# A gated-GELU feed-forward on one core: a 4-byte tile moves into the padding of the identity's tile, so that the SBUF pools start at multiples of 512 bytes

## The chip, the core and the metric

The kernel runs on one core of a Trainium2 chip. The metric is the device time of one execution in microseconds. Five engines work side by side and wait for each other through semaphores: PE (TensorE, matrix products), DVE (VectorE), ACT (ScalarE), POOL (GpSimd) and SP (SyncE, which here issues nearly all DMA transfers). PE appears twice in the profile: PE is the matrix product, PEld is the loading of the stationary operand ("the weights") that comes before each product. A product streams the other operand ("the moving operand") past those weights.

## The reference

```
B, S, Dm, Df = 1, 2048, 1024, 3584          # all inputs bfloat16
g = jnp.einsum("bsd,df->bsf", x, w_gate)
u = jnp.einsum("bsd,df->bsf", x, w_up)
h = _gelu(g) * u                            # tanh form of GELU
return jnp.einsum("bsf,fd->bsd", h, w_down)
```

## The kernel before, in words

The 2048 rows of x are taken in two passes (L1140) of two blocks of 512 rows each. For the first two products the 3584 hidden columns are cut into 14 units of 256 columns (`w_gate` and `w_up` are loaded by `load_w`, L151). The kernel does not multiply block by block in the plain way: it cuts rows, columns and the contraction in two and uses a scheme with seven products in place of eight. The scheme needs sums and differences of blocks: of x (t1 to t4, made by DVE, `sums_t`, L168), of the weights (s1 to s4, made mostly by POOL, `sums_s`, L183), and copies in 32 bits (tb, sa, made by ACT). They are kept in 32 bits (`f32r` in the code; the profile writes f32 or fp32r). So PE has two kinds of products of 128x512: bf16 with bf16, and f32 with f32. `matmul` (L144) issues every one of them, so all carry line L145. Units 4 to 13 go a level deeper (`pair0` L375, `pair1` L519). Then `down` (L898) multiplies the hidden values by `w_down` with the same scheme; in the last pass it calls `apart` (L866), whose products have five blocks K1, K3, K4, K22, K2 as weights (`load_ti`, L772). K1 and K2 are put into the two tiles `xT0` and `xT1`, which x no longer needs; K22, K3 and K4 go into tiles of the pool "w". Later in the same pass `make73` (L666) puts the first eight of fourteen moving blocks `tb` into `xT1` and `xT0` again (L675), and the other six into slots of the pool "k" (L679).

The order on PE, DVE, POOL, SP and ACT is that of the program text (L82 and the blocks under it); an agenda written by hand (L804 to L838) gives the step at which each load and each sum of `down` is made. Data passes from engine to engine by semaphore waits that the language derives from the tiles.

The pools of SBUF are opened in a fixed order (L83 to L89): x, m, h, w, k, s. Each takes the bytes behind the one before it, in every partition, rounded up to 32 bytes. Constants and a reserved part take the first 16,512 bytes. The pool x holds `hx` (1024 bytes, L294), `ident` (256 bytes, L996), `xT0` and `xT1` (8192 bytes each, L93) and `seen` (4 bytes, L1085). `ident` is the identity with which the first four row blocks of x are transposed (L1011). `seen` is written by POOL alone (`pool_behind`, L198) and read by nobody: the copy of one value makes POOL wait until DVE has made a tile, twice in the whole program (L1213).

From the sizes follow the places in the built program, in bytes of a partition (in brackets the rest after division by 512):

| tile or pool | before | after |
|---|---|---|
| hx | 16512 (128) | 16512 (128) |
| ident, or small | 17536 (128) | 17536 (128) |
| xT0, xT1 | 17792, 25984 (384) | 17920, 26112 (0) |
| seen | 34176 (384) | in small |
| m, two tiles of 6144 | 34208 (416) | 34304 (0) |
| hT | 46496 (416) | 46592 (0) |
| forms, hL | 83360 (416) | 83456 (0) |
| w, three tiles of 8192 | 103840 (416) | 103936 (0) |
| k, 36 slots of 2048 | 128416 (416) | 128512 (0) |
| s, 13 slots of 2048 | 202144 (416) | 202240 (0) |

Within a pool every tile is a multiple of 512 bytes long, and every operand of PE that is cut out of an f32 tile starts a multiple of 512 bytes behind the tile's start (128 columns of 4 bytes). So one rest holds for all f32 operands of a pool.

Of the kernel before, what the change touches and what calls it, by code (L numbers as in the profile page):

```python
# [10 lines left out]
def kernel(  # L11
# [26 lines left out]
    P = nc.NUM_PARTITIONS  # L38
    bf16 = mybir.dt.bfloat16
    f32 = mybir.dt.float32  # L40
# [42 lines left out]
    xpool = ctx.enter_context(tc.tile_pool(name="x", bufs=1))  # L83
# [909 lines left out]


    warm = nc.const_aps.tensor(1.0, [P, N], bf16)
    ident = xpool.tile([P, P], bf16, name="ident")  # L996
    make_identity(nc, ident)

    def load_x(c):
# [82 lines left out]
        s.make("sa", "s2", "s4")  # L1082
        t.make("t1")

    seen = xpool.tile([P, 1], f32, name="seen")  # L1085

    def rest_of_0(part):
        if part == 0:
# [244 lines left out]
```

## Time and profile before

| what | value |
|---|---|
| time, median of 3 runs | 535.11 us (534.42 to 536.17) |
| time of the profiled execution | 534.34 us |
| its span, from the first to the last instruction | 532.5 us |
| granted TensorE clock | 1.00 |
| PE busy | 527.3 us, 99% of the span, 2375 products |
| DVE, ACT, POOL busy | 404.6, 302.2, 268.2 us |
| DMA moved | 126.09 MB, mean 237 GB/s |

The profiled execution took 1.84 us more than its span (534.34 less 532.5): that is what lies ahead of the first and behind the last profiled instruction. The profile says how long each engine was busy, which chain of work ended last, and what ended each wait. Busy PE does not tell how densely the products follow each other, since they overlap; for that one takes the starts of products that follow each other.

### The profile page before, as it was taken

What the parts mean: (1) busy time and instruction counts of PE and PEld (TensorE: products, weight loads), DVE (VectorE), ACT (ScalarE), POOL (GpSimd) and SP (SyncE); (2) the same over time, 40 slices, a digit from 0 to 9 for tenths busy, and PEclk for the clock granted to TensorE, in tenths of its full rate; (3) what the DMA queues carried; (4) which work ended last, traced back from release to release, by engine and by line L of the source; (5) the groups of instructions that cost most, each with busy time, mean ns of one, the idle gap of its engine ahead of it and who ended that gap; (6) DMA issues with size and microseconds to landing.
All of it is one profiled execution on the core that took longest, in us unless ns stands there. A gap on an engine that the chain in (4) does not pass through costs nothing.

```text
span 532.5 us, 7751 instructions
## 1 busy us (share of the span) xinstructions
PE 527.3 (99%) x2375; PEld 373.7 (70%) x2375; DVE 404.6 (76%) x646; ACT 302.2 (57%) x545; POOL 268.2 (50%) x259
## 2 busy tenths in 40 slices
PE   8999999999999999999999999999999999999997
PEld 4568686867677774588886676767668674587885
DVE  2998768787777786938799877576576679789895
ACT  2557686868586851015556866566656651074580
POOL 1169976979797970000002989695978900000000
PEclk9999999999999999999999999999999999999999
DMA  9695318686777599999999799954383399499983
GB/s 246 153 254 170 87 60 295 199 296 199 236 226 257 186 361 369 387 293 267 225 276 295 246 281 350 324 153 140 99 225 97 118 370 353 159 342 337 217 191 131
DMA packets 140729, 126.09 MB, mean 237 GB/s; under 512 B 31632, under 2 KB 119184, under 8 KB 140560
## 3 DMA queue, kind: packets, MB, share of 16 engines
q1 hardware_dynamic: 136336, 124.55, 76.9%
q10 hardware_dynamic: 4352, 1.05, 1.5%
q8 instruction: 19, 0.31, 0.3%
q14 instruction: 22, 0.18, 0.1%
HBM read 86.38 MB, written 31.06 MB: 221 GB/s over the span
## 4 chain that ended last, share of the span: by engine, by line
PE 97%; DVE 2%; DMA 1%; SPq 0%; issue 0%; ACT 0%
PE bank L145 96%; DVE q L121 1%; DMA xn<-in_x_dram 1%; DVE xT L121 1%; SPq L1004 0%; PE bank L1011 0%; DVE st L854 0%; ACT st L853 0%
## 5 line engine op out<-in xcount | busy, mean ns | idle before, releaser
L124 POOL TENSOR_TENSOR s<-w 128x512 fp32r<-128x512 bf16 x102 | 117.4, 1169 | 47.5 <-DMA w<-in_w_gate_dram 37.0
L145 PE MATMUL bank<-t,s 128*128 128x512 f32 x528 | 126.3, 392 | 0.0
L145 PEld LDWEIGHTS bank<-t,s 128*128 128x128 f32 x528 | 99.0, 188 | 21.6 <-POOL s L124 0.3
L145 PE MATMUL bank<-xT,w 128*128 128x512 bf16 (+1 forms) x504 | 110.4, 376 | 0.0
L145 PEld LDWEIGHTS <-w 128*128 128x128 bf16 x504 | 47.8, 98 | 58.2 <-issue 4.2
L213 ACT ACTIVATE g<-sum 128x512 f32<-128x512 f32 x81 | 51.5, 636 | 60.1 <-DVE sum L121 59.3
L138 ACT COPY p<-bank 128x512 f32<-128x512 f32 x98 | 55.0, 589 | 46.6 <-PE bank L145 46.5
L121 DVE TENSOR_TENSOR hT<-g,bank 128x512 bf16<-128x512 f32 x72 | 49.0, 687 | 17.8 <-ACT g L213 12.2
L124 POOL TENSOR_TENSOR s<-w,s 128x512 fp32r<-128x512 bf16 x50 | 57.8, 1173 | 0.4
L124 POOL TENSOR_TENSOR s<-s,w 128x512 fp32r<-128x512 f32 x50 | 57.3, 1165 | 0.2
L145 PE MATMUL bank<-q 128*128 128x512 f32 x224 | 56.3, 391 | 0.1
L121 DVE TENSOR_TENSOR bank<-bank,p 128x512 f32<-128x512 f32 x74 | 51.3, 695 | 5.7 <-PE bank L145 5.1
L145 PE MATMUL bank<-t,sa 128*128 128x512 f32 x216 | 54.9, 397 | 0.0
L199 POOL COPY seen<-t 128x1 f32<-128x1 f32 x2 | 0.4, 183 | 107.8 <-DMA ti<-td 91.7
L145 PE MATMUL bank<-tb,s 128*128 128x512 f32 x216 | 54.3, 393 | 0.0
L145 PEld LDWEIGHTS bank<-q 128*128 128x128 f32 x224 | 42.1, 188 | 9.6 <-DVE xT L121 0.6
L145 PEld LDWEIGHTS bank<-t,sa 128*128 128x128 f32 x216 | 40.6, 188 | 9.1
L145 PEld LDWEIGHTS bank<-tb,s 128*128 128x128 f32 x216 | 40.5, 188 | 9.0 <-POOL s L124 0.3
L121 DVE TENSOR_TENSOR sum<-bank,p 128x512 f32<-128x512 f32 x54 | 37.0, 685 | 12.2 <-PE bank L145 11.1
L138 ACT COPY u<-bank 128x512 f32<-128x512 f32 x62 | 35.4, 595 | 17.5 <-PE bank L145 14.1
L133 ACT CAST tb<-raw 128x512 fp32r<-128x512 bf16 x20 | 12.0, 628 | 38.0 <-DMA raw<-in_w_down_dram 31.1
L133 ACT CAST sa<-w 128x512 fp32r<-128x512 bf16 x54 | 30.7, 617 | 3.4 <-DMA out_dram<-st 3.4
(123 smaller groups left out, 732.5 us busy)
## 6 DMA issues: line engine op xcount, KB each, us to landing
raw<-in_w_down_dram SPq DMA_DIRECT2D x72, 256.0 KB, 5.8
w<-in_w_gate_dram SPq DMA_DIRECT2D x27, 512.0 KB, 4.6
w<-in_w_up_dram SPq DMA_DIRECT2D x27, 512.0 KB, 6.1
td<-m SPq DMA_DIRECT2D x11, 768.0 KB, 5.3
q<-td SPq DMA_DIRECT2D x28, 256.0 KB, 5.4
pd<-xT SPq DMA_DIRECT2D x10, 512.0 KB, 5.9
w<-td SPq DMA_DIRECT2D x5, 1024.0 KB, 7.4
p<-pd SPq DMA_DIRECT2D x20, 256.0 KB, 4.7
```

The costliest lines, as they stand in the source:

```text
L121: nc.vector.tensor_tensor(out=out, in0=a, in1=b, op=op)
L124: nc.gpsimd.tensor_tensor(out=out, in0=a, in1=b, op=op)
L133: nc.scalar.copy(out=t, in_=src)
L138: nc.scalar.copy(out=t, in_=ps)
L145: nc.tensor.matmul(ps, lhsT=lhs, rhs=rhs, start=start, stop=stop, skip_group_check=True)
L199: nc.gpsimd.tensor_copy(out=seen, in_=tile[:, :1].bitcast(f32))
L213: nc.scalar.activation(g, src, ACT.Gelu_apprx_tanh)
```

## The change

```
-    ident = xpool.tile([P, P], bf16, name="ident")
+    small = xpool.tile([P, P + 64], bf16, name="small")
+    ident = small[:, :P]
     make_identity(nc, ident)
...
-    seen = xpool.tile([P, 1], f32, name="seen")
+    seen = small[:, P : P + 2].bitcast(f32)
```

The identity's tile grows from 256 to 384 bytes a partition, and the tile `seen` (4 bytes, 32 with its rounding) is no longer placed between `xT1` and the pool m; its value is written into two of the 64 new columns of the identity's tile. So `xT0` and `xT1` move up by 128 bytes and all pools behind them by 96 bytes. In the built program each of the five engines has the same instructions as before, in the same order and with the same semaphore waits; what differs is addresses.

## The prediction

> **What bounds the kernel now.** I read the page first: busy shares, then the chain that ended last.
>
> ```profile
> span 532.5 us, 7751 instructions
> PE 527.3 (99%) x2375; PEld 373.7 (70%) x2375; DVE 404.6 (76%) x646; ACT 302.2 (57%) x545; POOL 268.2 (50%) x259
> ...
> PE 97%; DVE 2%; DMA 1%; SPq 0%; issue 0%; ACT 0%
> ```
>
> PE is busy nearly all the time and 97% of the chain is its own work. Whether it ever waits is told by the busy time in stretches (columns: length, then PE, PEld, DVE, ACT, POOL busy, PE's clock, DMA share, GB/s).
>
> ```profile
> 7.33:120.00 112.67, 112.67 (x513) 77.04 (x514) 88.81 (x141) 75.24 (x139) 81.06 (x80) 1.00 0.67 194
> 120.00:240.00 120.00, 120.00 (x538) 84.02 (x537) 86.35 (x135) 60.36 (x114) 68.81 (x69) 1.00 0.85 280
> 240.00:360.00 120.00, 120.00 (x535) 88.06 (x534) 95.83 (x164) 76.95 (x147) 63.70 (x58) 1.00 0.93 267
> 360.00:482.80 122.80, 122.75 (x550) 83.86 (x548) 91.31 (x141) 63.51 (x111) 53.97 (x48) 1.00 0.68 218
> 482.80:529.04 46.24, 46.17 (x201) 37.66 (x201) 40.31 (x66) 22.17 (x32) 0.00 (x0) 1.00 0.89 219
> ```
>
> From 7.33 to 529.04 us PE lacks 0.12 us of being busy throughout, at full clock, though the DMA share goes from 0.67 to 0.93. So three things alone can move the end: the step from one product to the next on PE, the 7.33 us ahead of the dense part, and the 3.5 us behind it. The DVE pieces that the chain names between 474 and 483 us end in no wait of PE worth a name.
>
> Next, the steps. Busy times overlap, so I take starts from the timeline of PE (start, length, group, count) in two places of the last pass.
>
> ```profile
> 454.75 6.64 PE L145 MATMUL bank<-raw,hL 128*128 128x512 bf16 x30
> ...
> 463.98 6.69 PE L145 MATMUL bank<-s,xT 128*128 128x512 f32 x28
> 470.51 9.68 PE L145 MATMUL bank<-s,w 128*128 128x512 f32 x42
> 480.03 3.32 PE L145 MATMUL bank<-q 128*128 128x512 f32 x12
> ...
> 521.53 0.63 PE L145 MATMUL bank<-xT,q 128*128 128x512 f32 x2
> 522.00 1.53 PE L145 MATMUL bank<-tb,q 128*128 128x512 f32 x6
> 523.36 0.63 PE L145 MATMUL bank<-xT,q 128*128 128x512 f32 x2
> 523.83 1.53 PE L145 MATMUL bank<-tb,q 128*128 128x512 f32 x6
> ```
>
> bf16: 30 products last 6.64 us, the last one about 0.38 (a bf16 row's mean), so 29 steps of 215.9 ns. f32 with weights in the pool w: (480.03 - 470.51) / 42 = 226.7 ns. The same loop of `apart` with weights K1 and K2 in xT: (470.51 - 463.98) / 28 = 233.2 ns. In the last rows of `down` the moving block is in xT twice, then in a slot six times: 0.47 / 2 = 235 and 1.36 / 6 = 226.7 ns. The groups by shape (busy us, mean ns) say the same of all such products.
>
> ```profile
> L145 PE MATMUL bank<-tb,q 128*128 128x512 f32 x80 | 20.6, 389 | 0.0
> L145 PE MATMUL bank<-s,w 128*128 128x512 f32 x42 | 9.7, 389 | 0.0
> L145 PE MATMUL bank<-xT,q 128*128 128x512 f32 x32 | 9.1, 396 | 0.0
> L145 PE MATMUL bank<-s,xT 128*128 128x512 f32 x28 | 6.7, 395 | 0.0
> ```
>
> So 60 products are 6 to 7 ns slower, and they are just those of the 1606 f32 ones (the sum of the f32 counts by shape) whose operands have unequal rests after division by 512: 384 in xT, 416 in every other pool. It does not matter which of the two is in xT. The product just behind the last K2 weights shows it once more: in the trace the step whose running product has its own weights at 384 but the next weights at 416 is 227 ns. What counts seems to be the moving operand and the weights that are loaded meanwhile. bf16 products show no such thing: xT with w and raw with hT both step by 216 ns.
>
> **The change, part by part.** Instructions, order and waits stay; the costs are those of new addresses.
>
> *PE, f32.* After the change every pool has rest 0, so the two operands agree in all 1606 products, as they now do in 1546. I expect the 60 to take the 226.7 ns of the others: 28 x 6.5 = 0.18 and 32 x 6.6 = 0.21, together **-0.39 us**. All of them lie behind 463 us in a stretch where PE does not wait, so this comes off the end in full. The 1546 move by 96 bytes, with both operands together. No row shows an f32 pair with rests equal and other than 416, so this is the unknown. Bounds from the nearest rows: down to the bf16 step (10.8 ns less), up to the step of unequal rests (6.5 ns more) or twice that. I take 0, because of all rows the 1546 are nearest: equal rests then and now, and what the 60 show goes by the difference of the two.
>
> [...]
>
> *PE, bf16.* 712 full products at 216 ns whether the moving rest is 384 or 416: 0.
>
> *Start.* The chain in order of time has one DMA piece.
>
> ```profile
> 2.13 4.31 DMA xn<-in_x_dram
> ...
> 7.33 466.98 PE bank L145 x2094
> ```
>
> It is the first megabyte of x, in packets of 2048 bytes. In the trace's packets the median is 46 ns for 1 KB, 84 for 2 KB, 159 for 4 KB, 309 for 8 KB: 9.4 ns for each 256 bytes and 9 ns that do not depend on size. If these 9 ns were the price of the present rest and vanished, the piece would shrink by 9/84, or 0.46 us; if they doubled, it would grow as much. I take **-0.2 us**, between nothing and the gain, since a rounder start is not likely to lengthen a packet.
>
> [...]
>
> *All other DMAs, DVE, ACT, POOL.* 0. PE hides them: it waits 0.12 us in 521. If transfers got slower, POOL would be late first; PEld's waits name POOL's sums s twice, 0.6 us in all, so there is little slack there. Rows give no sign of a change: ACT reads xT at 617 ns (tb) and w at 617 (sa); DVE writes xT in 684 and sum in 685; ACT's copies into xT take 593, into u 595.
>
> *`seen`.* POOL's copy, 183 ns each, twice, with the same waits; the last reader of the identity is done by 7.3 us. 0. *Tail.* The last store is 128 KB; by the same 9 ns a packet it moves by under 0.1 us. 0.
>
> Sum against the profiled execution: 534.34 - 0.39 - 0.2 = 533.75 us. That execution was 0.77 us below the median of the runs shown, so against the median: 535.11 - 0.6 = **534.5 us**.
>
> **Rivals.**
>
> *A, small gain, as above:* 533.4 to 535.9 with the scatter of the runs. For: the control pairs in one and the same loop. Against: nothing shows rest 0.
>
> *B, all f32 products become faster (faster).* The 10.8 ns by which an f32 step exceeds a bf16 step might themselves be the price of starts that are multiples of 32 only. Whole price: 1546 x 10.8 + 60 x 17.3 = 17.7 us, so 517.2 with the start; half of it gives 526. For: the same 10.8 ns on all 1546, and bytes per column are what differs between the kinds. Against: 384 is a multiple of 128, rounder than 416, and goes with slower steps, not faster.
>
> *C, round starts collide (slower).* What costs 6.5 ns might be an operand that starts at a multiple of 128 bytes, in either role, and not the difference. Then the change charges the 1546 that pay nothing now: 1546 x 6.5 = 10.0 us, 544.9 with the start; with both operands charged, 20.5 us. It decides from about 1 ns a product on (1.6 us in all). For: 384 fits as well as the difference does. Against: it needs the same price by chance in both roles, and a round start that harms.
>
> *D, nothing.* The 60 are slow for another reason (xT's place near the bottom of the memory): 535.0. Against: xT1 reaches to 34,176, next door to the pool m, whose 32 products take 389 ns.
>
> **How the numbers follow.** A 0.62, D 0.04, B 0.22, C 0.12. A measurement of this kernel can tell about 0.3% (1.6 us) from no change. A and D fall within it: same 0.66; faster 0.22; slower 0.12. The range leaves out C whole and the part of B below 522 (0.06): 522 to 537; A's own is 533.4 to 535.9.
>
> **What would show it.** Right: the rows with xT fall from 395 and 396 to 389, the starts behind 463 us give 226.7 ns in all f32 groups, 4.31 us becomes about 4.1, and packets of 512 and 2048 bytes take 9 ns less or the same. Wrong: an f32 step in the pools w, k and s (s,w; tb,q) other than 226.7 ns. Each 1 ns there is 1.5 us, and everything else is small beside it.

## The result, and the profile after

Over 20 runs each, the changed kernel takes 534.15 us (median; 533.47 to 535.13) and the kernel before 534.76 us (534.36 to 537.04). The ratio is 0.9982 with a 95% interval of 0.9975 to 0.9990, that is 0.5 to 1.3 us less (the medians differ by 0.61 us, the means by 0.93). It is a small gain, clear of noise and within the 0.3% that the prediction called no change. The forecast was 0.6 us less (534.5 against a median of 535.11).

The profiled execution after took 534.37 us with a span of 532.6 us, no less than before (534.34 and 532.5). So one pair of profiles does not show the gain as a shorter span; it has to be looked for in its parts. First the page after, the same lines as before:

```profile
span 532.6 us, 7751 instructions
...
PE 527.6 (99%) x2375; PEld 374.0 (70%) x2375; DVE 405.0 (76%) x646; ACT 303.0 (57%) x545; POOL 268.3 (50%) x259
...
PE 92%; DMA 5%; DVE 2%; SPq 0%; ACT 0%; issue 0%
```

PE is the bound as before, but in this execution 5% of the chain is DMA. The share of the DMA queue fell as well, before and then after:

```profile
q1 hardware_dynamic: 136336, 124.55, 76.9%
```

```profile
q1 hardware_dynamic: 136336, 124.55, 74.5%
```

The steps first. PE's timeline after, in the same two places of the last pass (start, length, group, count):

```profile
464.54 6.51 PE L145 MATMUL bank<-s,xT 128*128 128x512 f32 x28
470.88 9.68 PE L145 MATMUL bank<-s,w 128*128 128x512 f32 x42
480.40 3.33 PE L145 MATMUL bank<-q 128*128 128x512 f32 x12
...
521.67 0.61 PE L145 MATMUL bank<-xT,q 128*128 128x512 f32 x2
522.12 1.52 PE L145 MATMUL bank<-tb,q 128*128 128x512 f32 x6
523.49 0.62 PE L145 MATMUL bank<-xT,q 128*128 128x512 f32 x2
523.94 1.52 PE L145 MATMUL bank<-tb,q 128*128 128x512 f32 x6
```

With weights K1 and K2 in xT the step is now (470.88 - 464.54) / 28 = 226.4 ns, where it was 233.2; with weights in the pool w it is (480.40 - 470.88) / 42 = 226.7, as it was. The two products with their moving block in xT take 0.45 us, where they took 0.47. By the trace's starts the means are 226.7 ns for the 32 and 226.7 for the 28 (before: 233.9 and 233.3), and the groups by shape have 389 ns throughout:

```profile
L145 PE MATMUL bank<-tb,q 128*128 128x512 f32 x80 | 20.6, 389 | 0.0
L145 PE MATMUL bank<-s,w 128*128 128x512 f32 x42 | 9.7, 389 | 0.0
L145 PE MATMUL bank<-xT,q 128*128 128x512 f32 x32 | 8.9, 389 | 0.0
L145 PE MATMUL bank<-s,xT 128*128 128x512 f32 x28 | 6.5, 389 | 0.0
```

So PE's own work became shorter by 32 x 7.2 + 28 x 6.6 ns = 0.42 us. What took it back in this one execution is in the chain in order of time:

```profile
203.80 6.70 DMA raw<-in_w_down_dram
210.50 0.05 issue
210.54 264.14 PE bank L145 x1180
```

At 210.54 us PE waited for a block of `w_down`: the step there lasts 554 ns instead of 216, so 0.34 us were lost. In the profile before, the block in this place had landed at 208.45 us, and PE came to it at 210.00 us, about 1.5 us later.

### The profile page after: what moved, and what is told of

The parts are those of the page before. It is cut to its first block, busy times and chain, and to the rows that moved or that the text cites. A ratio compares the mean times of both kernels' runs of the same rounds, so it can differ in the third digit from the quotient of the medians.

```text
span 532.6 us, 7751 instructions
## 1 busy us (share of the span) xinstructions
PE 527.6 (99%) x2375; PEld 374.0 (70%) x2375; DVE 405.0 (76%) x646; ACT 303.0 (57%) x545; POOL 268.3 (50%) x259
## 3 DMA queue, kind: packets, MB, share of 16 engines
q1 hardware_dynamic: 136336, 124.55, 74.5%
## 4 chain that ended last, share of the span: by engine, by line
PE 92%; DMA 5%; DVE 2%; SPq 0%; ACT 0%; issue 0%
PE bank L145 92%; DMA raw<-in_w_down_dram 2%; DMA hL<-w 1%; DVE q L121 1%; DMA xn<-in_x_dram 1%; DVE xT L121 1%; PE bank L1012 0%; SPq L618 0%; ACT xT L138 0%; SPq L1005 0%; SPq L689 0%; DVE st L854 0%; ACT st L853 0%
## 5 line engine op out<-in xcount | busy, mean ns | idle before, releaser
L124 POOL TENSOR_TENSOR s<-w 128x512 fp32r<-128x512 bf16 x102 | 117.4, 1170 | 46.3 <-DMA w<-in_w_gate_dram 35.5
```

The costliest lines, as they stand in the source:

```text
L124: nc.gpsimd.tensor_tensor(out=out, in0=a, in1=b, op=op)
```

## The experiments

**The changed kernel once more (after_again)**, for a second profile.

> The changed kernel once more, for a second profile and for a time beside the next runs on one chip. All theories: ratio to before 0.997 to 1.000. Steps of the f32 products with xT 226.7 ns. If the wait of PE for a block of w_down near 210 us (0.34 us in the first profile of the changed kernel) is chance, it is absent or of another length here; if it belongs to the change, it is there again with about 0.3 us.

533.93 us against 534.68 for before on the same chip; ratio 0.9983 (0.9974 to 0.9991). No wait of PE at 210 us: from the first full bf16 product (8.94 us) to the last start (528.28 us) there are 519.34 us, against 519.76 before and 519.68 - 0.34 = 519.34 in the first profile after. So the wait comes in one execution and not in the other, and the 0.42 us of PE are there both times.

**The 4-byte tile ahead of xT (seen_first)**: rest 416 for all pools, no round start anywhere.

```
     ident = xpool.tile([P, P], bf16, name="ident")
+    seen = xpool.tile([P, 1], f32, name="seen")
...
-    seen = xpool.tile([P, 1], f32, name="seen")
```

> The kernel before with the 4-byte tile placed ahead of xT instead of behind it: xT moves by 32 bytes to rest 416, where all other pools stay. No pool starts at a multiple of 512 or 256. Theory 'difference' (a product is slow when its moving operand and the next weights have unequal rests): the 60 products with xT step by 226.7 ns, 0.39 us less than before. Theory 'round starts' (the change helps because starts become multiples of 512): they stay at 233 to 235 ns. Theory 'packets' (the rest of the gain comes from DMA packets that start at multiples of 256): of the 512-byte packets 45% stay in the band of 32 to 39 ns as before, and the time lies between before and the changed kernel, ratio 0.999; if packets are worth nothing the ratio is that of the changed kernel.

The groups on PE, and the DMA queue's share, of seen_first:

```profile
L145 PE MATMUL bank<-xT,q 128*128 128x512 f32 x32 | 8.9, 389 | 0.0
L145 PE MATMUL bank<-s,xT 128*128 128x512 f32 x28 | 6.5, 389 | 0.0
```

```profile
q1 hardware_dynamic: 136336, 124.55, 77.3%
```

The same 389 ns without one round start: "round starts" falls, and so does rival D, since xT moved by 32 bytes only. In time it gives 534.36 us, ratio 0.9993 (0.9983 to 1.0003), some 0.4 us less than before but not the whole of the change's gain: its median is 0.43 us above that of after_again on the same chip.

**The pool s moved by 32, 64, 128 and 256 bytes (s_off_32, s_off_64, s_off_128, s_off_256)**, on the changed kernel:

```
+    gap = ctx.enter_context(tc.tile_pool(name="gap", bufs=1)).tile([P, 32], mybir.dt.uint8, name="gap")
     spool = ctx.enter_context(tc.tile_pool(name="s", bufs=SUMS))
```

> The changed kernel with 32 unused bytes ahead of the pool s: its 13 tiles (weights s1 to s4 and others) get rest 32, all other pools keep 0. In 907 of the 1586 pairs of an f32 product and the f32 weights loaded behind it the rests then differ. Theory 'difference': these step by 233 ns, 907 x 6.5 = 5.9 us more, about 540.0, ratio to before 1.010. Theory 'place' (xT alone is slow, as it lies near the bottom of the memory): nothing, ratio 0.998.

> As s_off_32, with 64 unused bytes ahead of the pool s. Theory 'any difference not a multiple of 256': the 907 pairs step by about 233 ns. Theory 'difference within a stretch of 64 bytes' (32 bytes apart is bad, 64 is as good as 0): they step by 227 ns as with 256.

> As s_off_32, with 128 unused bytes. Theory 'any difference not a multiple of 256': about 233 ns. Theory 'difference within a stretch of 64 bytes', and that of 128 bytes as well: 227 ns.

> As with 32, but 256 unused bytes: rest 256 for the pool s, 0 for all others, and every start is still a multiple of 256. Theory 'difference after division by 512': 907 slow products, 5.9 us more, ratio to before 1.010. Theory 'difference of small starts' (it matters where in a stretch of 256 bytes or less the two start): no slow product, ratio 0.998.

| bytes | pairs that differ | their step, mean | PE, first full bf16 product to last start | time | ratio to before |
|---|---|---|---|---|---|
| 0 (after_again) | none | 227.2 ns (all) | 519.34 us | 533.93 us | 0.9983 (0.9974 to 0.9991) |
| 32 | 907 | 233.1 ns | 525.14 us | 539.47 us | 1.0087 (1.0065 to 1.0108) |
| 64 | 907 | 233.0 ns | 525.96 us | 540.67 us (one run) | |
| 128 | 907 | 232.8 ns | 525.00 us | 540.32 us (one run) | |
| 256 | 907 (by 256) | 227.2 ns | 519.42 us | 533.87 us | 0.9984 (0.9974 to 0.9994) |

The means leave out the steps of 280 ns or longer, of which every kernel has 20 to 30. The timeline of PE shows the price in place. First s_off_32, then s_off_256; tb with s differs by the offset, forms with r (both outside the pool s) does not.

```profile
101.60 2.03 PE L146 MATMUL bank<-tb,s 128*128 128x512 f32 x8
103.47 1.07 PE L146 MATMUL bank<-forms,r 128*128 128x512 f32 x4
```

```profile
101.53 1.98 PE L146 MATMUL bank<-tb,s 128*128 128x512 f32 x8
103.34 1.07 PE L146 MATMUL bank<-forms,r 128*128 128x512 f32 x4
```

Eight steps take 1.87 us (234 ns each) with 32 bytes and 1.81 us (226) with 256. "Place" falls, since no tile of s is near the bottom. "Difference" holds, with one correction: it is the difference after division by **256**, not 512; 32, 64 and 128 bytes apart cost the same. The price nearly adds up: 907 x 5.9 ns (233.1 - 227.2) = 5.4 us, and the 670 equal pairs of s_off_32 average 228.3 ns, another 0.7 us, for which the runs show no reason. The steps of 280 ns or longer give 0.4 us back: near 482 us, where PE waits for DVE, the longest step becomes 419 ns instead of 561, and four steps of some 300 ns near 300 us are gone. That makes 5.7 us of the 5.8 us that the dense part lost (525.14 - 519.34).

Which weights count, those loaded next or the product's own, these runs leave open. By the addresses of the built program 48 of the steps have the next weights alone at another rest, and 42 their own alone. With 32 bytes they average 234.3 and 232.3 ns, with 64 bytes 227.6 and 230.6, with 128 bytes 233.0 and 231.8; steps with neither have 228.1, 228.9 and 228.2. So the next weights alone do not decide it.

**All pools at rest 128 or 256 (all_128, all_256)**: pairs equal, only DMA can tell.

```
-    small = xpool.tile([P, P + 64], bf16, name="small")
+    small = xpool.tile([P, P + 128], bf16, name="small")      # all_256: P + 192
```

> The changed kernel with the identity's tile 128 bytes longer: all pools from xT on have rest 128. Pairs on PE agree, so by theory 'difference' no step is slow. Theory 'packets care for 256 bytes': of the 512-byte packets some 45% last 29 ns or longer, as before the change, and the time is that of seen_first (ratio to before 0.9993); theory 'packets care for 64 or 128 bytes': 98% last 27 ns or less, ratio 0.998.

> The changed kernel with the identity's tile 256 bytes longer: all pools from xT on have rest 256. No step on PE is slow. Theory 'packets care for 256 bytes': 98% of the 512-byte packets last 27 ns or less, ratio to before 0.998, as the changed kernel. Theory 'packets care for 512 bytes': the band of longer ones is there, ratio 0.9993.

| kernel | rest of all pools | 512-byte packets at 27 ns or less | their mean | time | ratio to before |
|---|---|---|---|---|---|
| before | 416, xT 384 | 56% | 30.5 ns | 534.68 us | |
| seen_first | 416 | 55% | 30.5 ns | 534.36 us | 0.9993 (0.9983 to 1.0003) |
| all_128 | 128 | 62% | 30.0 ns | 534.91 us (before: 535.00) | 0.9999 (0.9987 to 1.0011) |
| all_256 | 256 | 99% | 27.7 ns | 534.06 us (before: 535.00) | 0.9987 (0.9978 to 0.9995) |
| after_again | 0 | 99% | 27.6 ns | 533.93 us | 0.9983 (0.9974 to 0.9991) |

The page's queue lines, all_128 and then all_256:

```profile
q1 hardware_dynamic: 136336, 124.55, 77.0%
```

```profile
q1 hardware_dynamic: 136336, 124.55, 74.0%
```

Packets of 512 bytes have a median of 27 ns in every kernel. What starts off a multiple of 256 adds is a band of 28 to 41 ns, which holds two packets in five (43% before, under 1% after). "Packets care for 256" holds and "for 512", "for 64 or 128" fall. In time the four kernels with round starts and equal pairs lie at 0.9982 to 0.9987, the two with equal pairs alone at 0.9993 and 0.9999. Some of the intervals overlap. Set beside each other on one chip, all_256 is 0.85 us below all_128 in the median (11 runs each) at equal steps on PE. So starts at multiples of 256 are worth something beside PE's steps, between the 0.4 us of seen_first against after_again and these 0.85, and the packets are what the traces show to go with them; the size is not measured well. By PE's part all_128 should lie 0.4 us below before; its interval (0.7 us less to 0.6 more) neither shows nor excludes that.

**Where that gain sits (late_128, late_256)**: 70 warming products instead of 7 (NWARM, L60), so that the first loads have landed before PE needs them.

> all_128 with 70 warming products in place of 7 ahead of the first transposes, so that PE turns to x only some 14 to 27 us after the start, when the first loads have landed; it is slower by that much. To be set against late_256, not against the kernel before. Theory 'start' (what 256-byte starts gain beside PE, and most of the scatter, comes from the first loads): late_128 and late_256 have the same median to within 0.3 us, and each scatters by less than 0.8 us. Theory 'late loads in the middle' (PE waits now and then for a load of the down product, 0.3 to 0.5 us a time): late_128 stays 0.5 to 0.9 us above late_256, with the scatter of before (some 1.5 us).

> The same 70 warming products on all_256. Theory 'start': the same median as late_128 to within 0.3 us, small scatter. Theory 'late loads in the middle': 0.5 to 0.9 us below late_128.

547.82 us (547.24 to 548.35) and 547.70 us (546.47 to 548.97), five runs each. The medians agree to 0.12 us, as "start" said, but the runs scatter by 1.1 and 2.5 us, which it did not. The profiles say why the pair cannot decide: the 70 products took 17.12 us in late_128 and 18.19 us in late_256, because PE's step fell from 427 to 219 ns after 8 products in one and after 13 in the other. And late_128 waits in the middle, which speaks for the other theory:

```profile
223.97 8.06 DMA raw<-in_w_down_dram
232.07 20.59 PE bank L145 x91
252.65 4.29 DMA q<-td
256.99 231.27 PE bank L145 x1032
```

Two steps of 0.79 and 0.80 us stand at the ends of these DMA pieces; late_256 has nothing of the kind, and its dense part is 1.3 us shorter (519.34 against 520.66 us). all_128 had one such step, 0.48 us at 243.2 us. But the first profile after had one as well, and before and seen_first had none. So this is left open.

One place outside the dense part does show in the traces: the wait of PE's weight load for the first block of `w_up`, which comes in packets of 512 bytes. Before and then after, in PEld's timeline (in brackets the wait and what ended it):

```profile
7.33 6.61 PEld L145 LDWEIGHTS <-w 128*128 128x128 bf16 x39 [0.28 <-DMA w<-in_w_up_dram]
```

```profile
7.48 6.61 PEld L145 LDWEIGHTS <-w 128*128 128x128 bf16 x39 [0.20 <-DMA w<-in_w_up_dram]
```

In the three profiles with 7 warming products whose pool w is off a multiple of 256 (before, seen_first, all_128) this wait is 0.28 to 0.32 us, in the seven others 0.15 to 0.20. That is about 0.13 us of the gain.

## Why the prediction was right

*The bound.* Right. PE's steps carry the result; in s_off_32 5.9 ns on 907 of them made the dense part 5.8 us longer and the median 5.5 us (539.47 against 533.93 in after_again). But "it waits 0.12 us in 521" was read from busy times, and these overlap (389 ns a product at a step of 227). The starts show that PE loses 0.44 us near 482 us (steps of 560 and 335 ns in place of 227, with busy times of 457 and 497), where the weight loads wait for the DVE pieces that the prediction set aside; in the waits of before this is

```profile
PEld bank L145 <- DVE xT L121: 0.6, 2, 0.4
```

The steps are 563 and 337 ns after the change, so this did no harm to the forecast.

*PE, f32, the 60: -0.39 us.* Right: 0.42 measured, in both profiles after and in seen_first. The mechanism was the forecast one, the agreement of the moving operand's start with that of the weights; "after division by 512" has to read 256, and that it is the weights loaded next was argued from one step and is not shown (see the s_off kernels). In the 907 pairs of s_off_32 the step is 233.1 against 227.2 ns.

*The 1546: 0.* Right: 226.7 ns at rest 416, 0, 128 and 256, so B (which needed less) and C (more) fall.

*Start: -0.2 us.* The step that failed in its mechanism. It took the 9 ns that packets cost apart from their size as the possible price of the rest. They are no such thing: the 2048-byte packets of x have a median of 84 ns before and after, and 417 against 423 of the 512 have just that. The piece of the chain became no shorter. In the first profile after it belongs to the third block of x, before and in after_again to the fourth:

```profile
1.66 4.37 DMA xn<-in_x_dram
```

```profile
2.13 4.50 DMA xn<-in_x_dram
```

The fourth block takes 4.50 us in after_again for 4.31 before; in the other kernels where the chain names it, it is 4.2 to 5.3 us, with no order by the rest. What the start did gain, about 0.13 us, lies at the first weights and their 512-byte packets, which the term did not have. The boundary that the runs show for these is 256 bytes: 62% of them take 27 ns or less in all_128, 99% in all_256. Their median, 27 ns, did not move.

*All other DMAs: 0, hidden by PE.* Too simple. The cover is thin near 210 us: the same load was 1.5 us early before, 0.3 us early in seen_first, and cost 0.34 us in the first profile after. What the round starts took off the queue's share (76.9% to 74.5%) is likely what brings the measured 0.96 us (0.5 to 1.3) above PE's 0.42; 0.13 us of it are at the first weights, and where the rest enters is not known.

*`seen`, ACT, DVE, POOL: 0.* Right; POOL's copy takes 184 ns for 183, ACT's tb 629 for 628 and sa 616 for 617, POOL's sums 1170 for 1169.

So the forecast total of -0.59 lies inside the measured interval, with one term right, one of about the right sign but put at the wrong load, and one that the forecast set at 0. That the sum comes so near is in part luck.

## What to carry to other kernels

Where a kernel hangs on the step of its 32-bit products, look at where their operands start. Here a difference of 32, 64 or 128 bytes between the starts of the moving rows and of the weights cost 6 ns a product and one of 256 bytes nothing; with 907 products hit it was 1% of the kernel (540.67 against 535.00 us in s_off_64), and one 4-byte tile behind `xT1` had set 60 products 32 bytes apart (0.42 us). Starts at multiples of 256 bytes also took the slow part off the DMA packets (the mean of the 512-byte ones goes from 30.5 to 27.7 ns); the one place where the traces show PE gaining by it is the wait for the first block of `w_up`, 0.13 us. Compare the starts of successive instructions, group by group, before a small effect is called noise: a row of 396 beside one of 389 ns was the whole sign.

## What the runs showed of the hardware

That 32, 64 and 128 bytes of difference cost the same 6 ns in the mean (233.1, 233.0 and 232.8 ns) and 256 nothing was not expected. bf16 products showed no price for a difference: w at 416 with xT at 384 stepped by 216 ns before, and by 216 with both at 0. And PE's step at the beginning falls from 427 to 219 ns after a time that differs between executions: 3.4 us and 5.6 us of products in the last two kernels. In the twelve profiles the granted clock becomes full 2.7 us (s_off_64) to 5.6 us (late_256) after the first product. The slower steps reach the start of the kernel itself: the same 16 transposes, before and then after, in PE's timeline, took

```profile
3.71 1.14 PE L1011 MATMUL bank<-ident,xn 128*128 128x128 bf16 x16
```

```profile
3.71 1.70 PE L1012 MATMUL bank<-small,xn 128*128 128x128 bf16 x16
```

Of the 0.56 us between them, about 0.3 are the clock (full from 3.88 us on before and from 4.89 after; a step of 107 ns lasts for one or two products before and for seven after, then it is 56), and most of the rest is a wait for the second block of x, which landed at 4.09 us before and at 4.68 after. Neither went further here: the next transposes began 0.05 us behind the landing of their rows in both. Only in all_256 did they begin later than that (rows at 5.25 us, transposes at 5.66); there the first 16 stand in the chain that ended last, with 1.68 us. The first full bf16 product comes at 8.5 to 9.7 us in the ten profiles with 7 warming products, 2.3 to 2.5 us behind the landing of the fourth block of x, and it is this landing, at 6.1 to 7.4 us, that scatters.
